# Cached attention decode: from two heads a step in double slots to four heads a step in single slots

## The chip, the cores and the metric

The kernel runs on one core of one Trainium2 chip. The metric is the device time of one execution in microseconds (us). The profiler's span, from which all stretches below are read, is about 2 us shorter than the time (before: 658.7 us of span, 660.75 us of time for the same execution).

## The reference, cut to what matters

```python
# x: [2, 1, 512], k_cache and v_cache: [2, 32, 8192, 128] bf16 (134 MB each)
xn = layernorm(x)
q  = (xn @ wq)                                    # 2 x 32 heads of 128
p  = softmax(q . k_cache * 128**-0.5)             # over 8192 keys
o  = p @ v_cache
return x + o.reshape(2, 1, 4096) @ wo + relu(xn @ w1) @ w2
```

64 heads with one query each read 268 MB of K and V once; with the weights it is 280.5 MB. There is little arithmetic per byte. The work for TensorE lies in the layout: keys arrive with the key index on the partitions, so each 128x128 block of K is transposed before the scores are formed.

## The kernel before

It takes two heads per step (64 partitions each, 128 keys per partition, rows of 32 KB), 32 steps. Two K slots and two V slots of 32 KB per partition, and a separate buffer for the weights:

```python
R = 2; EG = 8; NG = 16; REP = 32
...
ks = [sb([P, SLOT], bf16, f"ks{i}") for i in range(R)]
vs = [sb([P, SLOT], bf16, f"vs{i}") for i in range(R)]
w_sb = sb([P, max(WJ * D, KT * Dff + FJ * D)], bf16, "w_sb")
kT = [sb([P, EG, P], bf16, f"kT{i}") for i in range(4)]
```

SyncE issues all large loads on one queue. K for step t+2 is issued when the transposes of step t have been read, V for step t+1 when the weighted sums of step t-1 (which use the other slot) are done:

```python
load_k(0); load_k(1); load_v(0)
for t in range(NP - 2):
    sp.wait_ge(pT[HG - 1], 2 * (t + 1)); load_k(t + R)
    sp.wait_ge(sW, t + 1);               load_v(t + 1)
```

A step on TensorE transposes and scores pair t and runs the weighted sums of pair t-1. The softmax of pair t (maximum on VectorE, exponentials on ScalarE) runs beside these sums:

```python
for e in range(NG):
    transposes(r, e)                  # 8 transposes into PSUM; VectorE or ScalarE copies them to kT
    if e >= 2: scores(r, e - 2, h)    # 8 matmuls of 64 columns
...
for e in range(2, NG):
    weighted(v, e)                    # v = 1 - r: the pair before
    if e == 5: ...                    # maxima across partitions
    if e == 8: ...                    # broadcast of the maximum
```

The feed-forward part runs at the start, while K(0) loads; its weights come first in the queue.

## Time and profile before

| | before |
|---|---|
| time, median (range), 4 runs | 660.95 us (660.81 to 661.47) |
| bytes read | 280.50 MB |
| HBM rate, mid-run | 432 GB/s |
| TensorE busy | 559.4 us (85%) |
| VectorE, ScalarE busy | 253.2 us, 255.9 us (under 40%) |
| TensorE clock, mean | 0.94 |

The way to read it is the share of the DMA engines: it is full from the first slice to the last but one, so the time is the bytes at 432 GB/s plus both ends. TensorE's 85% says nothing by itself; it waits a little for K in nearly every step (68.7 us in all), and that wait is the sign of who is the bound. The prediction below shows the lines. In them PE is TensorE's matmuls and PEld its weight loads, DVE is VectorE, ACT ScalarE, POOL GpSimd and SPq SyncE's queue; the bracket gives the engine's idle time before the instruction and what ended it. "Warm" and "cold" mean that TensorE was granted its full clock (1.00) or half of it (0.50).

### The profile page before, as it was taken

The numbers are of one execution on the slowest core, as the hardware profiler recorded it, in microseconds if no ns is written. First come the engines' busy times: TensorE is split into PE (matmuls) and PEld (weight loads), VectorE is DVE, ScalarE is ACT, GpSimd is POOL, SyncE is SP. The second block draws the span as 40 slices with busy tenths as digits, with TensorE's granted clock in tenths as the row PEclk, the third lists the DMA queues.
The fourth block names the chain that finished last, engine by engine and source line by source line (L and its number), as shares of the span: only waits on it lengthen the run. The fifth ranks groups of instructions, "written<-read, shape, count | busy, mean of one in ns | idle before, by whom it ended". The sixth has DMA issues, their size and how long they took to land.

```text
span 658.7 us, 26862 instructions
## 1 busy us (share of the span) xinstructions
PE 559.4 (85%) x12737; PEld 536.4 (81%) x12737; DVE 253.2 (38%) x436; ACT 255.9 (39%) x403; POOL 9.0 (1%) x46
## 2 busy tenths in 40 slices
PE   2897799997889978789878878987978898878897
PEld 0497798987889878789878878987878898878896
DVE  1144344443434433334433434442434443434341
ACT  1043444443433534244353434443433434433340
POOL 1000000000000000000000000000000000000000
PEclk9889999998998989899988989897999988989996
DMA  8999999999999999999999999999999999999996
GB/s 365 431 442 418 439 430 431 434 426 438 424 442 426 436 430 430 436 426 438 424 440 432 430 432 428 438 424 442 422 440 430 430 436 424 440 424 440 432 422 279
DMA packets 10542, 280.66 MB, mean 426 GB/s; under 512 B 1186, under 2 KB 1188, under 8 KB 1700
## 3 DMA queue, kind: packets, MB, share of 16 engines
q1 hardware_dynamic: 10528, 280.50, 99.1%
q8 instruction: 9, 0.15, 0.1%
q14 instruction: 1, 0.01, 0.0%
q10 hardware_dynamic: 4, 0.00, 0.0%
HBM read 280.50 MB, written 0.00 MB: 426 GB/s over the span
## 4 chain that ended last, share of the span: by engine, by line
DMA 58%; PE 37%; ACT 2%; issue 1%; SPq 1%; ACTq 0%; DVE 0%
DMA ks<-in_A_k_cache_dram 54%; PE tp L302 22%; PE Sc L309 11%; PE ot L322 4%; DMA w_sb<-in_A_wo_dram 4%; ACT kT L431 1%; ACT L431 1%; SPq L193 0%; PE Sc L357 0%; SPq L188 0%; PE Sc L360 0%; SPq L176 0%; SPq L175 0%; SPq L169 0%; PE ot L413 0%
## 5 line engine op out<-in xcount | busy, mean ns | idle before, releaser
L302 PE MATMUL tp<-identb,ks 128*128 128x128 bf16 x4096 | 323.3, 228 | 68.7 <-DMA ks<-in_A_k_cache_dram 68.7
L431 DVE COPY kT<-tp 128x1024 bf16<-128x1024 bf16 x320 | 219.7, 691 | 325.6 <-PE tp L302 325.4
L302 PEld LDWEIGHTS tp<-identb,ks 128*128 128x128 bf16 x4096 | 254.8, 102 | 72.5 <-DMA ks<-in_A_k_cache_dram 72.4
L431 ACT COPY kT<-tp 128x1024 bf16<-128x1024 bf16 x192 | 194.3, 1012 | 231.6 <-PE tp L302 231.6
L309 PE MATMUL Sc<-q,kT 128*128 128x64 bf16 x4096 | 216.9, 196 | 7.2 <-ACT kT L431 5.7
L309 PEld LDWEIGHTS Sc<-q,kT 128*128 128x128 bf16 x4096 | 178.6, 100 | 10.8 <-ACT kT L431 9.1
L322 PE MATMUL ot<-prm,vs 128*128 128x64 bf16 x4224 | 157.6, 193 | 5.0 <-issue 5.0
L322 PEld LDWEIGHTS ot<-prm,vs 128*128 128x128 bf16 x4224 | 140.5, 98 | 7.9 <-issue 5.2
L537 ACT COPY nm<-Sc 128x2 f32<-128x2 f32 x32 | 5.1, 160 | 118.1 <-PE Sc L360 118.1
L541 ACT ACTIVATE prm<-Sc,nm 64x128 bf16<-64x128 f32 x64 | 25.6, 400 | 4.3
L482 DVE TENSOR_REDUCE mcol<-Sc 64x1 bf16<-64x128 f32 x64 | 18.7, 291 | 18.3 <-PE Sc L309 17.8
L431 ACT ACT_TABLE_LOAD x16 | 20.5, 1283 | 2.4 <-issue 2.4
L257 PE MATMUL ot<-vs,xz 128*16 128x512 bf16 x32 | 8.5, 434 | 8.7 <-DMA vs<-in_A_wq_dram 8.7
L532 ACT COPY OTf<-ot 128x2 f32 x32 | 5.1, 160 | 27.7 <-PE ot L322 27.7
L487 DVE TENSOR_REDUCE mx<-Sc 1x2 bf16<-1x128 bf16 x32 | 8.9, 279 | 16.9 <-PE Sc L357 16.9
L257 PEld LDWEIGHTS ot<-vs,xz 128*16 128x16 bf16 x32 | 3.1, 99 | 13.7 <-issue 10.8
L242 POOL COPY q<-qb 128x2 bf16<-128x2 bf16 x32 | 5.9, 187 | 590.0 <-PE Sc L309 568.1
L541 ACT ACTIVATION_READ_ACCUMULATOR prm<-Sc,nm x64 | 11.8, 185 | 0.0
L461 DVE TENSOR_SCALAR qs<-ot 16x512 bf16<-16x512 f32 x1 | 0.7, 678 | 17.1 <-PE ot L257 17.1
L357 PE MATMUL Sc<-identb,mcol 128*1 128x128 bf16 x32 | 7.0, 217 | 0.0
L360 PE MATMUL Sc<-mx,onesb 1*128 1x2 bf16 x32 | 5.5, 172 | 0.0
L413 PE MATMUL ot<-OX,w_sb 128*128 128x2 bf16 x128 | 4.0, 166 | 1.2 <-DMA w_sb<-in_A_wo_dram 0.7
(56 smaller groups left out, 38.1 us busy)
## 6 DMA issues: line engine op xcount, KB each, us to landing
ks<-in_A_k_cache_dram SPq DMA_DIRECT2D x32, 4096.0 KB, 26.7
vs<-in_A_v_cache_dram SPq DMA_DIRECT2D x31, 4096.0 KB, 31.3
vs<-in_A_wq_dram SPq DMA_DIRECT2D x1, 4096.0 KB, 12.3
vs<-in_A_v_cache_dram SPq DMA_DIRECT2D x2, 2048.0 KB, 19.0
w_sb<-in_B_w_dram SPq DMA_DIRECT2D x2, 1792.0 KB, 18.0
w_sb<-in_A_wo_dram SPq DMA_DIRECT2D x1, 1792.0 KB
w_sb<-in_A_wo_dram SPq DMA_DIRECT2D x1, 896.0 KB, 26.8
w_sb<-in_A_wo_dram SPq DMA_DIRECT2D x1, 768.0 KB, 28.2
```

The costliest lines, as they stand in the source:

```text
L242: g.tensor_copy(q2[t % R][:], qb[:, 2 * t:2 * t + 2]).then_inc(sQ1, 1)
L257: i = pe.matmul(qp, lhsT=xz[:, kt, Z - g * Bsz:Z - g * Bsz + QG * Bsz], rhs=vs[1][:, (kt * QG + g) * 512:(kt * QG + g + 1) * 512], start=( ...
L302: t = pe.transpose(tp[e % 4][:, i, :], ks[r][:, kk * Dh:(kk + 1) * Dh], identb[:])
L309: t = pe.matmul(Sc[r][:, 2 * kk:2 * kk + 2 * REP], lhsT=kT[e % 4][:, i, :], rhs=rep(q2[r][:]), start=True, stop=True,)
L322: t = pe.matmul(ot[r][:, 0:2 * REP], lhsT=vs[r][:, kk * Dh:(kk + 1) * Dh], rhs=rep(prm[r][:, kk, :]), start=(kk == 0), stop=(kk == KB - 1),)
L357: pe.transpose(tr_of(r), mcol[r][:], identb[:]).then_inc(sT, 1)
L360: pe.matmul(bc_of(r), lhsT=onesb[:], rhs=mx[r][:], start=True, stop=True).then_inc(sB, 1)
L431: fn(kT[e % 4][:], tp[e % 4][:]).then_inc(kR[e % HG], 1)
L482: m = v.tensor_reduce(out=mcol[i][half, :], in_=S_of(i)[half, :, u], axis=AX.X, op=ALU.max)
L487: v.tensor_reduce(out=mx[i][:], in_=tr_of(i).rearrange("o (u m) -> o u m", u=2), axis=AX.X, op=ALU.max, negate=True,).then_inc(sX, 1)
L532: a.copy(OTf[:, bass.ds(c, 2)], ot[r][:, 0:2]).then_inc(sO, 1)
L541: x = a.activation(out=prm[i][half, :, u], in_=S_of(i)[half, :, u], func=ACTF.Exp, bias=nm[i][half, u:u + 1], scale=1.0, accum_out=RS[half ...
```

## The change

The intent: half as many, larger steps. Four heads share a step (32 partitions each, 256 keys per partition, rows of 64 KB). The same slot memory then holds one K and one V slot. To free the K slot early, the transposed K of a whole step is kept (32 tiles of kT instead of 4), and most scores follow after the transposes. The feed-forward part moves to the end, its weights and wo into the K slot, so the weight buffer goes.

```diff
-R = 2
+U = 4
 EG = 8
-NG = 16
-REP = 32
+NG = 32
+REP = 16
+LAG = 28
+EARLY = 16
...
-    ks = [sb([P, SLOT], bf16, f"ks{i}") for i in range(R)]
-    vs = [sb([P, SLOT], bf16, f"vs{i}") for i in range(R)]
-    w_sb = sb([P, max(WJ * D, KT * Dff + FJ * D)], bf16, "w_sb")
-    kT = [sb([P, EG, P], bf16, f"kT{i}") for i in range(4)]
+    ks = sb([P, SLOT], bf16, "ks")
+    vs = sb([P, SLOT], bf16, "vs")
+    wo_sb = ks[:, 0:WJ * D]...            # w1, w2 behind it
+    kT = [sb([P, EG, P], bf16, f"kT{i}") for i in range(NG)]
...
+        for t in range(NP):
+            if t > 0:
+                sp.wait_ge(pT[HG - 1], NH * t)        # all transposes of step t-1
+            sp.dma_start(ks[:], K_all[rows, :])...    # (the last step's K in two halves)
+            ...
+                sp.wait_ge(sW, t)                     # all weighted sums of step t-1
+            sp.dma_start(vs[:], V_all[rows, :]).then_inc(dV, 16)
...
+            for e in range(NG):
+                ...
+                transposes(e)
+                if e >= LAG: scores(e - LAG)
+            for e in range(NG - LAG, NG): scores(e)
+            pe.wait_ge(sM, reg)  ... transposes of the maxima
+            pe.wait_ge(sX, reg)  ... broadcast
+            pe.wait_ge(sP, reg)                       # probabilities of this very step
+            pe.wait_ge(dV, n16)
+            for kk in range(KB): ... weighted sums
...
-    prm = [sb([P, KB, 2], bf16, f"prm{i}") for i in range(R)]
+    prm = sb([P, KB, U], bf16, "prm")
```

## The prediction

> **What bounds the kernel now.** I read the page's head and its DMA rows first, then the stretches, then one step of the timeline.
>
> ```profile
> span 658.7 us, 26862 instructions
> ...
> DMA  8999999999999999999999999999999999999996
> ...
> HBM read 280.50 MB, written 0.00 MB: 426 GB/s over the span
> ```
>
> The 16 DMA engines are full in every slice but the first and the last. Stretches (time, busy of PE, PEld, DVE, ACT and POOL, PE clock, DMA share, GB/s) give the rate and the start:
>
> ```profile
> 0.00:5.00 5.00, 0.24 (x4) 0.19 (x4) 2.13 (x9) 2.94 (x4) 3.12 (x14) 1.00 0.62 210
> ...
> 333.00:373.00 40.00, 34.26 (x772) 33.65 (x772) 15.56 (x26) 15.89 (x25) 0.37 (x2) 0.91 1.00 432
> ```
>
> So the steady rate is 432 GB/s: 4.19 MB take 9.71 us, and two heads (K and V) 19.4 us. Everything else hides behind that, because two K and two V slots keep at least one load queued. The timeline shows one two-head step:
>
> ```profile
> 334.20 2.74 PE L302 MATMUL tp<-identb,ks 128*128 128x128 bf16 x24 [3.42 <-DMA ks<-in_A_k_cache_dram]
> ...
> 336.74 0.63 PE L309 MATMUL Sc<-q,kT 128*128 128x64 bf16 x8
> ...
> 337.18 0.63 PE L302 MATMUL tp<-identb,ks 128*128 128x128 bf16 x8
> ...
> 339.29 0.61 PE L302 MATMUL tp<-identb,ks 128*128 128x128 bf16 x8
> ...
> 339.98 0.61 PE L302 MATMUL tp<-identb,ks 128*128 128x128 bf16 x8
> ...
> 346.17 0.33 SPq L164 DMA_DIRECT2D ks<-in_A_k_cache_dram  x1
> ...
> 347.40 0.60 DVE L482 TENSOR_REDUCE mcol<-Sc 64x1 bf16<-64x128 f32 x2 [0.53 <-PE Sc L309]
> ...
> 348.52 0.28 DVE L487 TENSOR_REDUCE mx<-Sc 1x2 bf16<-1x128 bf16 x1 [0.53 <-PE Sc L357]
> ...
> 349.46 0.16 ACT L537 COPY nm<-Sc 128x2 f32<-128x2 f32 x1 [3.67 <-PE Sc L360]
> 349.75 0.40 ACT L541 ACTIVATE prm<-Sc,nm 64x128 bf16<-64x128 f32 x1
> 350.02 0.19 ACT L541 ACTIVATION_READ_ACCUMULATOR prm<-Sc,nm  x1
> 350.21 0.40 ACT L541 ACTIVATE prm<-Sc,nm 64x128 bf16<-64x128 f32 x1
> ...
> 351.27 0.33 SPq L167 DMA_DIRECT2D vs<-in_A_v_cache_dram  x1
> ```
>
> TensorE waits 3.42 us for K, then works about 17 us on the step. Softmax (347.4 to 350.7) runs beside the weighted sums of the pair before: it costs TensorE nothing. K is issued for the slot just read while another K is already landing, hence 26.7 us from issue to landing for 9.71 us of data. All of this slack comes from the second slots and the shifted V work. The change gives up both.
>
> [...]So loads issued by SyncE run one after the other; the 26.7 us agree. [...]Here the first load is issued at 0.97 us; a DMA share of 0.62 in the first 5 us puts its start near 1.9, so 0.95 us from issue to flow. It is used at 13.35 (12.4 us after issue), so about 1.65 us from last byte to use. [...]after the 3.42 us wait, eight scores start 0.44 us ahead of the next group (336.74 to 337.18), where eight warm ones take 0.245; the cold stretch lasts about 3 us, and 40 us with two of them show a clock of 0.91.
>
> **The change, part by part.** Bytes are the same (280.5 MB). A step is now four heads: K 8.39 MB = 19.42 us, V the same, so DMA needs 38.84 us per step, exactly what two old steps need. 16 steps instead of 32.
>
> *Transposes (T).* A transposes-plus-scores pair of groups takes 0.693 us (339.29 to 339.98); scores alone 0.245; so 0.448 for eight transposes. 32 groups = 14.3 us, plus four score groups mixed in (1.0) = 15.3 us. The copies follow: DVE 20 x 0.692 = 13.8 us and ACT 12 x 1.012 = 12.1 us, just below. If TensorE starts cold, 3.4 us at half speed add 1.7: 17.0 us.
>
> *Scores (S)* that remain: 28 x 0.245 = 6.9 us.
>
> *Softmax (X),* now with TensorE idle. Semaphore and drain 0.2; four reductions of the second half at 0.30 (the pair above takes 0.60) = 1.2; two transposes with hops 0.45; maximum over 256 instead of 128 elements 0.28 + 0.13 = 0.41; broadcast and copy 0.55; four exponentials. Two of 128 elements start 0.46 us apart; 128 more at 0.83 ns (from ACT's 1012 ns for 1024 against 160 ns for 2) make 0.58, times four = 2.3. Sum with the last hop: 5.2 us.
>
> *Weighted sums (W).* 256 x 30.6 ns = 7.8 us, 8.0 with drain. But 5.2 us of idleness precede every one, longer than the wait that made the clock fall above: cold for 3.4 us, plus 1.7 = 9.7 us.
>
> *The loop.* From K(t)'s last byte at 0: V(t) flows until 19.42. TensorE starts at 1.65, ends T at 17.0 (18.7 cold); K(t+1) can flow 0.95 later, at 17.9 (19.6), so there DMA loses 0 to 0.2. K(t+1) ends at 38.8 to 39.0. W ends at 1.65 + 15.3 + 6.9 + 5.2 + 9.7 = 38.75 (40.45 cold), and V(t+1) flows from 39.7 (41.4). The DMA queue is empty for 0.9 (2.4) us. After a late W, T follows nearly at once and warm, V(t+1) still covers the next K's issue and that step loses nothing; so the loss comes every other step. Before the lossy steps TensorE has waited some 3.6 us for K, so the cold case is likely: 2.6 us per two steps, 40.15 us per step instead of 38.84. Warm: 39.3.
>
> *Ends.* K(0) lands at 0.97 + 0.95 + 12.58 MB / 432 + 1.65 = 32.7 us (before: the same, the feed-forward weights then came first). First-pass instruction stalls of TensorE (2.39 and 2.64 us in the old chain) are no longer hidden: +3. Last step about 37 us, less up to 2 from K's halves. After the last W: normalisation 1.9 with 56 feed-forward matmuls beside and after it, transposes, selection and copies 1, 56 + 128 matmuls at 27 ns (84 take 2.27 in the old tail) 5.0, output 3.3: about 12 us. The weights land in the K slot meanwhile (V(15) plus 7.86 MB, 18 us), hidden.
>
> Sum, likely case: 32.7 + 15 x 40.15 + 37 - 2 + 12 + 3 = 685 us; warm transposes 672; DMA full throughout (38.84): 32.7 + 582.6 + 35 + 12 = 662.
>
> **Rivals.** (a) *DMA stays full, same time:* for it, DVE and ACT are far from full and the sums miss 38.84 by only 1 to 2.6 us; against it, every margin is used once and the softmax bubble is new. 655 to 666 us[...]. (b) *TensorE becomes the bound at every step,* because the cold stretches are longer[...] or copies fall behind in T (DVE has only 0.5 us of slack in 14.3, and ACT reloads its table, 1.28 us, at each loop top): T + S + X + W near 41, 695 to 705 us. (c) *Larger rows make DMA faster:* [...]it can't pay for an idle queue.
>
> **Range and chances.** I weight the likely case most, shade it toward the warm one since my hop times are rounded up: 682 us, 8 in 10 from 664 to 697. Faster by over 2% needs 648 us[...]: 0.02. Within 2% (to 674) is rival (a) or the warm case: 0.28. Slower: 0.70.
>
> **What would show it.** DMA share in the middle near 0.96 to 0.98 instead of 1.00, GB/s near 417; SyncE's V issue waiting for the last weighted sum while no K is left in flight; TensorE idle 5 us per step before the weighted sums with the first of them at about double duration; a step of 40 us; mean PE clock near 0.90. Wrong if the DMA row stays at 1.00 in mid-run, if the softmax gap is under 4 us, or if T takes over 18 us.

## More of the kernel before

In the kernel before, the 0.50 of mid-run comes in stretches of 3.41 us, in two cases of 6.83; in the step that the prediction quotes it lasts from 333.82 to 337.23 us.

## The result, and the profile after

The changed kernel is correct and slower: 696.92 us median (694.67 to 697.19, 4 runs) against 660.95. The ratio is 1.0535 (95% interval 1.0513 to 1.0558). Ratios here are the mean time of one kernel's fast runs over that of the other's of the same rounds, so not quite the ratio of the medians quoted. Executions over 1.5% slower than the fastest of the same kernel are left out of the means.

The page's head of the changed kernel, its clock and DMA rows (tenths of each of 40 slices):

```profile
span 695.2 us, 26564 instructions
...
PEclk9796898989899898989979898998989898898987
DMA  9999499999999899998999999999999989998992
...
HBM read 280.50 MB, written 0.00 MB: 403 GB/s over the span
```

The same bytes, but the fifth slice shows a hole in the DMA row, and later slices show eights. The rate in mid-run, in the view of stretches (columns as in the prediction: time, busy of five engines, PE clock, DMA share, GB/s), first of the kernel before, then of the changed kernel:

```profile
100.00:580.00 480.00, 417.82 (x9731) 407.60 (x9729) 195.06 (x329) 199.71 (x314) 4.85 (x26) 0.95 1.00 432
```

```profile
120.00:600.00 480.00, 392.64 (x9252) 386.23 (x9252) 191.01 (x348) 200.18 (x275) 2.24 (x12) 0.90 0.98 419
```

A step in that timeline, from the K issue to the next transposes:

```profile
377.26 7.19 PE L272 MATMUL Sc<-q,kT 128*128 128x64 bf16 x232
377.45 0.33 SPq L169 DMA_DIRECT2D ks<-in_A_k_cache_dram  x1
...
384.49 1.20 DVE L441 TENSOR_REDUCE mcol<-Sc 32x1 bf16<-32x128 f32 x4 [2.70 <-PE Sc L272]
385.74 0.27 PE L303 MATMUL ms<-identb,mcol 128*1 128x128 bf16 x2 [1.29 <-DVE mcol L441]
386.05 0.41 DVE L446 TENSOR_REDUCE mx<-ms 1x4 bf16<-1x256 bf16 x1 [0.37 <-PE ms L303]
...
387.02 0.82 ACT L492 ACTIVATE prm<-Sc,nm 32x256 bf16<-32x256 f32 x1
...
387.85 0.82 ACT L492 ACTIVATE prm<-Sc,nm 32x256 bf16<-32x256 f32 x1
...
390.40 10.16 PE L311 MATMUL ot<-prm,vs 128*128 128x64 bf16 x256 [3.70 <-ACT prm L492]
400.59 0.33 SPq L178 DMA_DIRECT2D vs<-in_A_v_cache_dram  x1
...
400.73 1.46 PE L265 MATMUL tp<-identb,ks 128*128 128x128 bf16 x23 [0.17 <-DMA ks<-in_A_k_cache_dram]
```

The softmax chain that ran beside the weighted sums now stands before them: the scores end at 384.45, the sums begin at 390.40, 5.9 us later. They take 10.16 us for 256 matmuls, where 256 warm ones took 7.91 in run 6 below, and only their end lets the next V be issued. The chain of work that ended last was, before, 58% DMA and 37% TensorE; after:

```profile
PE 48%; DMA 47%; ACT 3%; issue 1%; DVE 1%; ACTq 0%; SPq 0%
```

Where the 36.5 us of span went, read from the V issues (each marks the end of a step's weighted sums) at 79.55 and 642.69 us. The need of DMA is 38.84 us per step:

| stretch | after | at DMA's pace | difference |
|---|---|---|---|
| K(0) usable | 32.6 us | 32.8 (before) | 0 |
| first step, to 79.55 | 47.0 | 38.8 | 8.1 |
| 14 steps, to 642.69 | 563.1 (40.22 each) | 543.8 | 19.4 |
| last step and the end, to 695.2 | 52.5 | 43.4 (what remains of before's 658.7) | 9.1 |

The trace's record of single DMA packets shows what a dry queue costs. For successive 8.39 MB loads of the changed kernel (times moved so that the first load's first packet falls at 1.95 us; that move is an assumption, so the leads below may be off by some tenths):

```
load    issued   first packet   last packet ends   duration   the load before ended
V(3)    158.84     159.75          180.24            20.5       159.16
K(4)    175.08     179.71          199.58            19.9       180.24
V(4)    197.17     199.09          218.91            19.8       199.58
K(5)    216.88     218.61          240.56            21.95      218.91
V(5)    240.08     240.99          261.59            20.6       240.56
```

K(4) and V(4) were queued in time: each moved the end of the queue on by 19.3 us. V(3) and V(5) were issued only 0.3 and 0.5 us before the queue ended; it stood empty for 0.4 to 0.6 us, and its end moved on by 21.1 and 21.0 us, 1.7 us too much each. K(5) was issued 2.0 us before V(4) ended, and the end still moved on by 21.65 us, 2.3 too much: between 218.6 and 220.2 us only 9 of the 16 engines, on average, carried a packet. Of the loads from K(2) to V(14) in this run, every one issued 2.1 us or less before the end of the queue paid 1.5 to 2.5 us, and every one issued 2.2 us or more before it paid 0.2 at most. The border is not a constant: in run 6 below a load issued 2.55 us before the end, K(10), still lost 1.6.

### The profile page after: what moved, and what is told of

It reads as the page before. It is cut to its first block, busy times and chain, and to the rows that moved or that the text cites. A ratio compares the mean times of both kernels' runs of the same rounds, so it can differ in the third digit from the quotient of the medians.

```text
span 695.2 us, 26564 instructions
## 1 busy us (share of the span) xinstructions
PE 548.6 (79%) x12635; PEld 533.6 (77%) x12635; DVE 259.7 (37%) x481; ACT 270.3 (39%) x371; POOL 7.1 (1%) x30
## 3 DMA queue, kind: packets, MB, share of 16 engines
q1 hardware_dynamic: 5776, 280.50, 94.5%
HBM read 280.50 MB, written 0.00 MB: 403 GB/s over the span
## 4 chain that ended last, share of the span: by engine, by line
PE 48%; DMA 47%; ACT 3%; issue 1%; DVE 1%; ACTq 0%; SPq 0%
DMA ks<-in_A_k_cache_dram 47%; PE tp L265 34%; PE Sc L272 6%; PE ot L311 6%; ACT prm L492 2%; PE Sc L365 1%; DVE mcol L441 1%; ACT L394 1%; PE ms L338 0%; ACT kT L394 0%; DVE mx L446 0%; PE ms L303 0%; PE Sc L324 0%; PE ms L306 0%; ACT nm L488 0%
## 5 line engine op out<-in xcount | busy, mean ns | idle before, releaser
L394 DVE COPY kT<-tp 128x1024 bf16<-128x1024 bf16 x320 | 211.0, 688 | 294.0 <-PE tp L265 288.5
L265 PE MATMUL tp<-identb,ks 128*128 128x128 bf16 x4096 | 248.9, 223 | 37.0 <-DMA ks<-in_A_k_cache_dram 34.3
L265 PEld LDWEIGHTS tp<-identb,ks 128*128 128x128 bf16 x4096 | 238.2, 100 | 39.7 <-DMA ks<-in_A_k_cache_dram 36.0
L311 PEld LDWEIGHTS ot<-prm,vs 128*128 128x128 bf16 x4096 | 152.5, 107 | 60.6 <-ACT prm L492 60.6
L272 PE MATMUL Sc<-q,kT 128*128 128x64 bf16 (+8 forms) x4096 | 136.6, 191 | 4.3 <-issue 4.3
L272 PEld LDWEIGHTS Sc<-q,kT 128*128 128x128 bf16 x4096 | 132.4, 98 | 4.5 <-issue 4.5
L441 DVE TENSOR_REDUCE mcol<-Sc 32x1 bf16<-32x128 f32 x128 | 37.1, 290 | 89.6 <-PE Sc L272 88.3
L492 ACT ACTIVATE prm<-Sc,nm 32x256 bf16<-32x256 f32 x64 | 52.4, 818 | 2.7
L303 PE MATMUL ms<-identb,mcol 128*1 128x128 bf16 x32 | 4.5, 222 | 20.7 <-DVE mcol L441 20.7
L306 PEld LDWEIGHTS ms<-mx,onesb 1*128 1x128 bf16 x16 | 1.5, 92 | 11.2 <-DVE mx L446 11.2
L446 DVE TENSOR_REDUCE mx<-ms 1x4 bf16<-1x256 bf16 x16 | 6.6, 413 | 5.9 <-PE ms L303 5.9
```

What stands on the lines that cost most here:

```text
L265: t = pe.transpose(tp[e % 4][:, i, :], ks[:, kk * Dh:(kk + 1) * Dh], identb[:])
L272: t = pe.matmul(Sc[:, U * kk:U * (kk + n)], lhsT=kT[e][:, i, :], rhs=rep(q4[:], n), start=True, stop=True,)
L303: t = pe.transpose(trp[:, i * P:(i + 1) * P], mcol[:, i:i + 1], identb[:])
L306: pe.matmul(bc, lhsT=onesb[:], rhs=mx[:], start=True, stop=True).then_inc(sB, 1)
L311: t = pe.matmul(ot[:, 0:U * REP], lhsT=vs[:, kk * Dh:(kk + 1) * Dh], rhs=rep(prm[:, kk, :], REP), start=(kk == 0), stop=(kk == KB - 1),)
L394: fn(kT[e][:], tp[e % 4][:]).then_inc(kR[e % HG], 1)
```

## The experiments

**Theory.** The slots are freed whole, so SyncE can issue the next load only at one instant per step, and TensorE's chain (transposes, scores, softmax gap, weighted sums) is as long as DMA's 38.84 us. Each late issue leaves DMA without work. **Rivals:** rows of 64 KB move slower; TensorE's chain alone is the bound in every step; the cold clock in the weighted sums is what makes the difference.

**1. Row size alone.** Slots, waits and order as in the changed kernel, each load in two transfers of 32-KB rows.

```diff
-            sp.dma_start(vs[:], V_all[rows, :]).then_inc(dV, 16)
+            for i, d in enumerate((dV, dVb)):
+                half = slice(i * SLOT // 2, (i + 1) * SLOT // 2)
+                sp.dma_start(vs[:, half], V_all[rows, half]).then_inc(d, 16)
```

(the same for K; TensorE waits for both halves before it starts.)

> Each K and each V load of the changed kernel is issued as two transfers of 32-KB rows, back to back, so the slots are freed and waited for exactly as before; only the row size changes. Theory (the queue runs dry because a whole slot must be free): 693 to 699 us, no change. Rival (64-KB rows move slower, the GB/s row shows 422 where it showed 430 to 440): the time falls to 680 us or less.

Measured: 693.42 us (690.17 to 695.88), ratio 1.0477. The profiled execution (695.88) is 1.3 us below the profiled one of the changed kernel (697.19). In it the first step is 3.5 us shorter (the sums end at 76.02 instead of 79.55; TensorE stood once on "issue", waiting for nothing the profile shows, for 1.8 us, in the changed kernel twice, for 0.5 and 3.8, and into the longer of these, 55.31 to 59.10 us, falls a packet of instructions), the next 14 steps together 2.0 us shorter, and the rest 4.3 us longer (56.8 us for 52.5). The steps stay at 40.1 us ((637.20 - 76.02) / 14), and the packets agree: 2.418 us for 64 KB, 1.213 for 32 KB. The row size is no cause.

**2. K slot by halves.** Only K changes: its first half is issued after 16 of the 32 groups of transposes.

```diff
+            for i, d in enumerate((dKa, dKb)):
+                if t > 0:
+                    sp.wait_ge(pT[HG - 1], NH * (t - 1) + (i + 1) * NH // 2)
+                half = slice(i * SLOT // 2, (i + 1) * SLOT // 2)
+                sp.dma_start(ks[:, half], K_all[rows, half]).then_inc(d, 16)
```

> K slot freed and refilled by halves (first half issued after 16 of 32 groups of transposes), V as in the changed kernel. Theory: K no longer lands after the weighted sums end, the wait for K goes in all but the first steps, the step becomes TensorE's own chain of 39.2 to 39.5 us, and the first transposes start 9.7 us earlier: 672 to 682 us. Rival (TensorE is the bound at every step already): only the earlier start, 685 to 690 us.

Measured: 675.31 us, ratio 1.0211 (1.0194 to 1.0228). As the theory had it: the steps are 39.24 us ((621.76 - 72.34) / 14), and TensorE's waits for K fall from 34.3 us in all to 2.5.

**3. V slot by halves.** Only V changes: the first half is issued half way through the weighted sums (SyncE's half of the edit, not shown, is as for K in run 2).

```diff
             for kk in range(KB):
+                if kk == KB // 2:
+                    t.then_inc(sWa, 1)
+                    pe.wait_ge(dVb, n16)
```

> V slot freed and refilled by halves (first half issued half way through the weighted sums), K as in the changed kernel. Theory: the queue is no longer empty at the end of the weighted sums, the step becomes 39.2 us, 680 to 686 us. Rival (TensorE is the bound at every step): unchanged, above 692 us.

Measured: 680.65 us, ratio 1.0309 (1.0283 to 1.0336): the theory's range. The bare TensorE rival falls with this run, since nothing in TensorE's chain changed and the steps went to 39.3 us ((622.08 - 111.69) / 13).

**4. Both slots by halves.**

> Both slots refilled by halves. Theory: no more than the K halves alone, because TensorE's chain of about 39.2 us a step is then the bound: 670 to 680 us, DMA share near 0.99 in mid-run. Rival (the two gaps add up and DMA is the only bound): 664 us or less.

Measured: 673.90 us, ratio 1.0190. In mid-run:

```profile
120.00:600.00 480.00, 402.45 (x9491) 395.97 (x9489) 196.44 (x359) 205.16 (x281) 2.24 (x12) 0.91 1.00 429
```

The steps are 39.20 us ((614.88 - 105.32) / 13); with K alone by halves they are 39.24, with V alone 39.26. The gains don't add up: once the queue is kept fed, TensorE's own chain, 0.4 us longer than DMA's, is the bound. In the changed kernel it was neither chain alone, but the two locked together through the whole slots.

**5. The softmax gap filled, first try.** 86 throwaway transposes keep TensorE busy, in three lots before its three waits.

```diff
+        def busy(n):
+            for _ in range(n):
+                pe.transpose(tp[3][:, 0, :], identb[:], identb[:])
...
+            busy(20)
             pe.wait_ge(sM, reg)
...
+            busy(6)
             pe.wait_ge(sX, reg)
...
+            busy(60)
             pe.wait_ge(sP, reg)
```

> 86 throwaway transposes into a free PSUM tile fill the softmax gap, so the clock of TensorE should stay up. Theory (DMA waits for a TensorE chain that the cold clock lengthens): the weighted sums fall from 9.4 to 10.3 us to about 8.1, the step from 40.1 to 38.9 to 39.6 us, the time to 673 to 686 us. Rival (DMA or the row size sets the pace, the cold clock is harmless): weighted sums shorter, time above 690 us.

Measured: 853.16 us, ratio 1.2914, 156 us above the changed kernel. Both expectations missed. The page's row for the queue that fetches instructions, first of the changed kernel, then of this one:

```profile
q8 instruction: 8, 0.13, 0.1%
```

```profile
q8 instruction: 144, 2.36, 1.2%
```

and its chain of waits and one turn of its timeline:

```profile
PE 72%; issue 20%; DMA 4%; DVE 3%; ACT 1%; SPq 0%; ACTq 0%
```

```profile
387.21 4.58 PE L265 MATMUL tp<-identb,ks 128*128 128x128 bf16 x50 [4.06 <-issue]
...
394.80 11.96 PE L265 MATMUL tp<-identb,ks 128*128 128x128 bf16 x182 [3.01 <-issue]
```

"issue" is time in which TensorE waited for nothing the profile shows. 136 more packets of 16 KB over the 15 later turns are 9 per turn: the loop is fetched again in every turn. The loop body grew from about 771 to 857 matmuls (each with a weight load), from about 1,540 to 1,710 such instructions, and only with the larger one do packets come in every turn. This says nothing on the clock.

**6. The gap filled with few, wide matmuls.** 5 + 1 + 15 matmuls of 512 columns, 21 in place of 86.

```diff
+                pe.matmul(tp[3][...].bitcast(f32), lhsT=identb[:],
+                          rhs=kT[0][...][:, 0:512], start=True, stop=True)
```

> The softmax gap of the changed kernel filled with 21 matmuls of 512 columns instead of 86 transposes of 128, the same array time with a quarter of the instructions. If the 160 us of the first filler came from instructions fetched again in every turn of the loop: few instruction packets as in the changed kernel (8, not 144), no issue waits after the first step, weighted sums near 8.1 us, 673 to 686 us. If even 42 more instructions are too many: above 800 us again, and the question of the clock stays open. If filling itself hurts (PSUM or SBUF traffic): no issue waits and still above 695 us.

Measured: 697.98 us median of four (688.71 to 702.38, the highest slow), so no better than the changed kernel except in the fastest of the four, which is the profiled one; even there the steps from 157.44 to 598.44 us take 40.1 us each. There are 8 instruction packets and no issue waits after the first step, as hoped: about 1,580 matmuls and weight loads in a turn are not fetched again, where 1,710 were. The clock is warm and the weighted sums are as short as expected, but:

```profile
106.99 7.91 PE L324 MATMUL ot<-prm,vs 128*128 128x64 bf16 x256 [0.37 <-ACT prm L505]
...
119.21 10.97 PE L265 MATMUL tp<-identb,ks 128*128 128x128 bf16 x156 [4.31 <-DMA ks<-in_A_k_cache_dram]
```

What the sums gained, about 2 us a step, goes into waiting for K (46.7 us in all, 34.3 in the changed kernel) and into transposes that start cold after it (clock 0.50 from 119.21 to 123 us). So the K issue comes late instead of the V issue. In the worst turn K is issued at 136.54, usable at 161.43 (24.9 us later), and its slot is free again at 178.16 (16.7 us later): 41.6 us around the K slot alone. The packets of that K took 23.9 us, 4 more than those of a load queued in time; it had been issued 1.6 us before the queue ended. The expectation of a gain failed here: the rival that the cold clock makes the difference falls, and my own claim that this chain could be shortened at any place. A shorter chain does not help while a whole slot has to be free.

**7. Both halves with the first filler.**

> Both slots by halves and the softmax gap filled. Theory: TensorE's chain falls to about 37.3 us, DMA is full again at 38.8 us a step, and what remains over the kernel before is the last step and the tail: 658 to 667 us. Rival (something else, such as instruction fetch or row size, costs time in every step): above 670 us.

Measured: 815.70 us, ratio 1.2343. A miss for the same reason (144 instruction packets), so no test of the theory.

**8. Both halves with the wide filler.**

> Both slots by halves, probabilities laid out as in the changed kernel, the softmax gap filled with the 21 wide matmuls. The weighted sums fall from 10.2 to 8.0 us, so TensorE's chain from 39.2 to about 37.2 us, under DMA's 38.84; with a half slot always free early, the queue does not run dry. Theory: steps of 38.8 to 39.0 us, 660 to 667 us; the rest over the kernel before is the last step and the tail. If something else than the two found limits (a slot freed whole, TensorE's chain) costs time in the steps: above 670 us.

Measured: 661.75 us (661.70 to 661.79), ratio 1.0012 (0.9996 to 1.0029), the same time as the kernel before.

```profile
120.00:600.00 480.00, 442.73 (x9818) 394.38 (x9816) 195.02 (x360) 205.55 (x286) 2.44 (x13) 1.00 1.00 432
```

Clock 1.00, DMA share 1.00, 432 GB/s: with the slots refilled by halves and TensorE's chain below 38.84 us, the four-head form runs at DMA's pace (V issues at 214.68 and 603.34, ten steps: 38.87 us each). TensorE's chain alone shows where it catches up after the first step: 37.1 and 37.3 us (V issues at 101.38, 138.52 and 175.84). The clock that gave nothing in run 6 gives 12 us here, because here TensorE's chain was the bound. This is the best version of the four-head form, and it does not beat the kernel before: both are bound by the same bytes.

**9. What slows the exponentials.** Its output is wrong, which doesn't matter for the time. It passed the comparison all the same, which shows only that the check is loose for it.

```diff
-                    out=prm[own, :, u],
-                    in_=S[own, :, u],
+                    out=<rows without gaps> if u == 1 else prm[own, :, u],
+                    in_=(S[own, :, 0], S[own, :, 1], Sc[own, 384:640], <every 2nd of Sc[own, 0:512]>)[u],
```

> Wrong result on purpose: the four exponentials of a step read and write differently, 256 elements each on 32 partitions. 0 as in the changed kernel (reads every 4th element over two banks, writes every 4th); 1 writes without gaps; 2 reads without gaps, across the bank border; 3 reads every 2nd element in one bank. If the read distance makes one take 0.82 us rather than the 0.51 I had worked out, 2 is near 0.5 and 3 between; if the write distance, 1 is near 0.5; if the bank border, only 3 is short; if it is the element count alone, all four stay near 0.82.

Measured (690.61 us, a single run, its state unknown): the four in order are

```profile
386.42 0.82 ACT L492 ACTIVATE prm<-Sc,nm 32x256 bf16<-32x256 f32 x1
...
387.25 0.47 ACT L492 ACTIVATE prm<-Sc,nm 32x256 bf16<-32x256 f32 x1
...
387.82 0.82 ACT L492 ACTIVATE prm<-Sc,nm 32x256 bf16<-32x256 f32 x1
...
388.66 0.82 ACT L492 ACTIVATE prm<-Sc,nm 32x256 bf16<-32x256 f32 x1
```

Only the one that writes without gaps is short. It is the distance of the writes (8 bytes between 2-byte elements), not the reads (0.82 us without gaps, at every 2nd and at every 4th element) and not the bank border (0.82 us across column 512 and within the first 512), that makes 0.82 of 0.47 us.

**10. Probabilities head by head,** so that all exponentials write without gaps.

```diff
-    prm = sb([P, KB, U], bf16, "prm")
+    prm = sb([P, U, KB], bf16, "prm")
...
-                    rhs=rep(prm[:, kk, :], REP),
+                    rhs=rep(prm[:, :, kk], REP),
```

> Probabilities stored head by head, so that each exponential writes without gaps (correct result). The four exponentials shrink from 0.83 to about 0.49 us apart, the gap before the weighted sums from 5.9 to 4.5 us. Theory: half of the 1.4 us shows in the steps where DMA is not late, all of it in the first and last step: 682 to 690 us. Rival (weighted sums read slower from rows 512 bytes apart): 695 us or more, with weighted sums over 11 us.

Measured: 972.63 us, ratio 1.4712. The exponentials are 0.47 us each, but:

```profile
411.82 28.46 PE L311 MATMUL ot<-prm,vs 128*128 128x64 bf16 x256 [2.64 <-ACT prm L492]
```

The weighted sums take 28.5 us, 111 ns a matmul, since their moving columns now lie 512 bytes apart; and the granted clock stays at 0.50 through all of it, although TensorE shows as busy. The clock is not what makes them long: in run 12 below the sums start at clock 1.00 (31 matmuls in the 3.28 us from 401.72) and go on at 0.50 (38 in the 4.00 us from 408.00), at the same pace. The rival had asked for over 11 us. The layout that slows ScalarE is the one TensorE needs: with the four heads side by side an exponential takes 0.82 us and the sums 10.16, with the heads 512 bytes apart 0.47 and 28.46. Why the distance costs TensorE so much was not shown.

**11 and 12. The same layout with both halves, and with the wide filler too.**

> Both slots by halves and the exponentials without gaps. TensorE's chain falls from 39.2 to about 37.8 us, below DMA's 38.84: DMA bound, and what remains is the first turn, last step and tail: 659 to 667 us. If TensorE still sets the pace 672 us or more.

> As the run before with the 21 wide fillers. DMA is the bound in mid-run, so the fillers only shorten the last step (about 2 us) and the catching up after the first: 655 to 664 us. If the 42 instructions bring the fetching back: above 780 us.

Measured: 962.43 us (ratio 1.4561) and 971.90 us (1.4721). Both miss for the reason of run 10: weighted sums of 28 us are the bound whatever the slots do. Neither tests the theory.

## Why the prediction was right or wrong

The direction and the mechanism were right; the time came out 15 us above the central 682 and 0.1 us below the upper end of the range, 697. That it still lies inside is luck: one of the four executions took 697.19.

- *Bytes and rate, no gain from rows.* Right: 280.50 MB, 64-KB packets at the pace of 32-KB ones, and run 1 shows no change in the steps. Rival (c) falls. The small chance for "faster" fits an estimate from the rate of the trace: at 432 GB/s 280.5 MB take 649 us, and 648 was needed.
- *Transposes, scores.* Right: 15.24 us warm (441.83 to 457.07) for 15.3, 16.9 cold (360.59 to 377.45) for 17.0, scores 7.0 for 6.9. ScalarE's table load at each turn (1.28 us) added about 1 us in steps that follow the sums at once (400.73 to 416.83, 16.1 us).
- *Softmax gap.* Mis-sized: 5.9 us for 5.2. The term was the four exponentials, 0.83 us apart for the 0.58 worked out, +1.0 us, because of the distance of the writes (run 9). The other terms, estimates, came out a little shorter (0.04 us from the last score, 384.45, to the first reduction, 384.49, for the 0.2 of "semaphore and drain").
- *Weighted sums.* Right: 9.1 to 10.4 us for 9.7, cold at the start. The cold stretch was twice the 3.4 us of the estimate, 6.83 us (388.8 to 395.6 in the step above), but 1.6 us of it lay in the gap.
- *The loop.* The sum was right, 40.22 us a step for 40.15, but it was composed differently. "There DMA loses 0 to 0.2" failed: a K issued 2.0 us before the queue ended cost 1.5 to 2.5 us, though only in every fourth step. The loss at a late V, every other step, was 1.5 to 2.4 us where 2.4 was forecast. The two errors cancel: from the end of V(5) to that of V(9), four steps, V(7), K(9) and V(9) lost 5.7 us together, for 5.2 in the forecast.
- *First step.* 47.0 us against the 43.15 in the sum (40.15 + 3). Two stalls on issue of 4.3 us together for 3, a cold start of the transposes (17.4), a gap of 6.0 and sums of 10.3 us.
- *Last step and end.* 52.5 us against 47 (37 - 2 + 12). The two halves of the last K brought nothing, because TensorE was in the sums before (until 642.6) when K landed: +2. The chain of that step, 38.7 us for 37, contains ScalarE's table load and the longer gap. In the end 56 feed-forward matmuls took 3.5 us, 62 ns each, for the 27 assumed: +2.
- *Span and time.* The sum was one of the span, named as time: +2 us. With these misses, 685 + 3.8 + 1.0 + 5.5 + 2 = 697. Two small slips in its figures change nothing: 12.4 us from issue to use leaves 1.7 us after the last byte, not 1.65, and the terms of the end add up to 11.2 us, not 12.
- *Shading to 682.* Wrong: hop times "rounded up" did not outweigh the terms left out.
- *Rivals.* (a) and (c) fall; that (c) "can't pay for an idle queue" was the author's estimate. (b), TensorE the bound at every step, is not what happened in the changed kernel (run 3), but becomes true once the queue is fed, at 39.2 us a step and not 41 (run 4).
- *What would show it.* DMA share 0.98 and 419 GB/s for 0.96 to 0.98 and 417; clock 0.89 for 0.90; a gap of 5.9 us for 5.

Shown by runs: row size is no cause; the whole-slot release is, and with it TensorE's chain (runs 2 to 4 and 8). Left open: why a load issued into an ending queue is slow for its first packets, which take up to 3.6 us instead of 2.42, and why some engines get theirs later. Not tried: taking the last step's and the end's 9 us apart. In run 8 they are still there (607.3 to 659.9, 52.6 us) and are made up at the other end: with K by halves the first transposes begin at 24.65 instead of 32.59, and the early steps, shorter than DMA's 38.84 us, catch up.

## What to carry to other kernels

Doubling the step in the same memory turns a double buffer into a single one: add up what stands between "slot read" and "slot needed again", and if that chain plus a load is near the loop's bound, release the slot in parts. Work that hid beside the previous step's work comes out into the open when the steps are not staggered any more; count it (5.9 us here), and count the clock that its idle time costs (10.16 us for the sums behind the idle gap, 7.91 with the gap filled, run 6). A shorter chain on an engine gives nothing until the buffer that gates the transfers is released early (run 6 against run 8).
